# Moving seven small load requests from ScalarE's queue to SP's in a decode kernel

## The chip, the cores and the metric

The kernel runs on one core of a Trainium2 chip. A core has a matrix engine (TensorE, PE), whose weight loads are listed separately (PEld), a vector engine (VectorE, DVE), an activation engine (ScalarE, ACT), GpSimd (POOL) and SyncE (SP). Transfers from the chip's main memory (HBM) into the core's memory are carried out by 16 DMA engines, and they are requested by instructions on SP or on ScalarE. The metric is the device time of one execution in microseconds (us); the median over several runs counts.

## The reference

One token of a decoder: attention over a long cache, a small token mixer, and a gate that blends the two.

```python
x = A_x                                              # [1, 1, 448]
g = sigmoid((x * gate_w).sum(-1, keepdims=True))     # one number

q = (x @ wq)                                         # wq [448, 4096]: 16 heads of 256
k, v = k_cache, v_cache                              # 8 heads, 65536 rows of 256 each; 2 query heads share one
p = softmax(q . k * 256 ** -0.5)
a = (p . v) @ wo                                     # wo [4096, 448]

h = layernorm(x)
u = gelu(h * w1 + b1)                                # w1, b1: 1792 numbers each; u is [448, 1792]
b = u @ w2 + b2                                      # w2: 1792 numbers, b2: one

out = g * a + (1 - g) * b
```

All inputs are bf16. The two caches are 268 MB each; everything else is small beside them.

## The kernel before

**Blocks.** Each of the 8 cache heads is cut into 4 blocks of 16384 rows, 8 MiB of keys and 8 MiB of values each: 32 blocks. For a block, VectorE transposes the keys (`transposes`, L410), TensorE forms the scores (`scores`, L418), a softmax step follows (`softmax`, from L475), and TensorE multiplies the probabilities with the values (`pv`, L438). A running maximum and a running denominator carry from block to block.

**The loop.** `For_i` at L605 runs 15 times over two blocks each. The last two blocks stand behind the loop, written out, with the last values loaded in seven pieces (`load_v_last`, L161). All engines meet at the loop's entry. In the loop SP requests the values of a block (`load_v`, L135) and then the keys of the next one (`load_k_whole`, L132); it waits for a place to come free ahead of each. The very first keys are requested ahead of the loop, the first values inside it.

**Places in memory.** The keys live in `k_all`, three half-block slots; block 0 takes the first two. The third slot is used before the loop as room for the mixer (`gel`, `xf`, `h_bc`, `zt`). The values live in `vt`. Before the first values come, `vt` holds `wq`: its first 384 rows (`wq_m`, 3 MiB) and the last 64 (`wq_t`, 512 KiB).

**Order.** Every instruction goes through `seq`, which ties it to the one before it on its engine, so that an engine's work runs in the order written. The start-up is written in this order:

- The loads. ScalarE requests x (`xr`, L166), three tables of 14 rows (`w1`, `b1` and `w2`, L176), the gate's weights in two halves (`gw`, L178) and b2 (`b2b`, L181). SP requests `wq_t` (L167), `wq_m` (L170) and the first keys (L132).
- Constants on GpSimd and VectorE (L185 to L226).
- x is brought into columns and spread over 128 rows by TensorE (L237 to L245), which needs `xr` and the constant `ones_b` (L212).
- One product turns the tables into columns (L263). VectorE copies the result out (L273, L274), directly after the first statistics of the layer norm, and then takes two Newton steps for the reciprocal root (L277 to L282) and forms `h_bc` (L283).
- ScalarE takes 14 Gelus from `h_bc` and the tables (L288).
- TensorE forms q from `wq` and x (L299, L306); it is spread into `qz` (L317 to L332).
- The gate's sum is taken (L346 to L348: it needs `gw`, and its Exp stands behind the Gelus on ScalarE), and TensorE sums the mixer (L352).
- `mixer_tail` (L357 to L368, which needs `b2b`) is written behind the loop, but in the trace it runs on VectorE before the loop is entered.

**Semaphores of the loads.** The ten loads ahead of the loop share eight semaphores in turn. A load that takes over the semaphore of an earlier one waits until that one has landed: the ninth for the first, the tenth for the second. The order of taking them follows the order of the loads: x, `wq_t`, the rest, with b2 as the ninth and the first keys as the tenth.

Of the kernel before, what the change touches and what calls it, by code (L numbers as in the profile page):

```python
# [33 lines left out]
def kernel(  # L34
# [15 lines left out]
    nc = tc.nc  # L50
# [5 lines left out]
    NF = F // 128  # L56
# [6 lines left out]
    def seq(ins):  # L63
        e = ins.ins.engine
        if e in last:
            tc.add_manual_dep(
                ins.ins,
                last[e],
                mybir.DependencyInfo(
                    mybir.DependencyClass.NoSync, mybir.DependencyReason.DATA  # L70
                ),
                reason="program order",
            )
        last[e] = ins.ins.name
        return ins
# [29 lines left out]
    xr = const.tile([1, D], BF16)  # L105
    gw = const.tile([1, D], BF16)
    tables = const.tile([3 * NF, 128], BF16)
    w2b = const.tile([128, NF], BF16)
    b2b = const.tile([1, 1], BF16)
# [21 lines left out]
    def load_k_whole(n, slot):  # L131
        seq(nc.sync.dma_start(out=k_all[:, slot * KP:(slot + 2) * KP, :], in_=rows("k", n)))  # L132
# [26 lines left out]
    def load_v_last(n):  # L159
# [3 lines left out]
                in_=rows("v", n)[:, j0:j1, :],  # L163
            ))

    seq(nc.scalar.dma_start(out=xr[:], in_=A_x[0, 0].rearrange("(o n) -> o n", o=1)))  # L166
    seq(nc.sync.dma_start(  # L167
        out=wq_t[:, :], in_=A_wq[DM:D, :].rearrange("r (h n) -> (r h) n", h=2)
    ))
    seq(nc.sync.dma_start(out=wq_m, in_=A_wq[0:DM, :].rearrange("(p k) n -> p k n", k=3)))  # L170
    for k, table in enumerate((
        B_w1[0].rearrange("(b p) -> b p", p=128),
        B_b1.rearrange("(b p) -> b p", p=128),
        B_w2.rearrange("(b p) o -> b (p o)", p=128),
    )):
        seq(nc.scalar.dma_start(out=tables[k * NF:(k + 1) * NF, :], in_=table))  # L176
    for n0, n1 in ((0, D // 2), (D // 2, D)):
        seq(nc.scalar.dma_start(  # L178
            out=gw[:, n0:n1], in_=gate_w.rearrange("(o n) -> o n", o=1)[:, n0:n1]
        ))  # L180
    seq(nc.scalar.dma_start(out=b2b[:], in_=B_b2.rearrange("(o n) -> o n", o=1)))  # L181
    load_k_whole(0, 0)


# [9 lines left out]
        out=val[:], in_=rowsel[:, :, :, 0:NI], op=ALU.add, axis=AXIS.XY  # L194
    ))
    fst = const.tile([128, 2, REP], FP32)
    for e in range(2):
        seq(nc.vector.tensor_reduce(
            out=fst[:, e, :], in_=rowsel[:, :, :, e:e + 1], op=ALU.add, axis=AXIS.XY
# [3 lines left out]
        out=par[:], in_=ident_f[:].rearrange("p (a r) -> p r a", r=REP), op=ALU.add, axis=AXIS.X  # L203
# [3 lines left out]
        out=nval[:], in0=val[:], scalar1=-scale, scalar2=None, op0=ALU.mult  # L207
# [7 lines left out]
        out=same[:], in_=val[:].unsqueeze(1).to_broadcast([128, 64, REP])  # L215
# [8 lines left out]
        out=sel[:],  # L224
        in_=ident.rearrange("p (w k) -> p w k", w=NW).unsqueeze(2).to_broadcast([128, NW, NQ, 32]),
# [7 lines left out]
        out=xrr[:], in_=xr[:, DM:D].unsqueeze(2).to_broadcast([1, D - DM, 2])  # L233
    ))
    x_col = hd_ps[:, 40:44]
    for k in range(3):
# [13 lines left out]
        out=xtm[:], in0=par[:], scalar1=x_col[:, 3:4], scalar2=None, op0=ALU.mult  # L250
# [19 lines left out]
        out=veps[:], in0=mv[:, 1:2], scalar1=1e-5, scalar2=None, op0=ALU.add  # L270
# [5 lines left out]
    for _ in range(2):  # L276
# [3 lines left out]
            out=ntmp[:], in0=ntmp[:], scalar1=-0.5, scalar2=1.5, op0=ALU.mult, op1=ALU.add  # L280
# [3 lines left out]
        out=h_bc, in0=xf, scalar1=mv[:, 0:1], scalar2=rstd[:, 0:1],  # L284
        op0=ALU.subtract, op1=ALU.mult,
    ))
    for b in range(NF):
        seq(nc.scalar.activation(  # L288
            out=gel[b], in_=h_bc, func=ACT.Gelu_apprx_tanh,
# [33 lines left out]
    for k in range(2):  # L323
        seq(nc.vector.tensor_copy(
            out=qq[:, :, :, k, :], in_=qq_ps.rearrange("p (w g r) -> p w g r", g=HKV, r=REP)
# [314 lines left out]
    for n in (L - 1, L):  # L640
# [14 lines left out]
        else:  # L655
            def rest_base():
# [9 lines left out]
                out=lsv[:], in0=val[:], scalar1=lsum[:, 0:1], scalar2=None, op0=ALU.mult  # L666
# [8 lines left out]
                out=rdv[:], in0=rdv[:], scalar1=gcol[:, 0:1], scalar2=None, op0=ALU.mult  # L675
# [6 lines left out]
    for c in range(2):  # L682
# [9 lines left out]
        out=oT[:], in0=o_last, in1=rdv[:].unsqueeze(1).to_broadcast([128, 2, REP]), op=ALU.mult  # L692
# [43 lines left out]
```

## Time and profile before

| | us |
|---|---|
| median of 3 runs | 1264.22 |
| lowest and highest | 1263.58, 1266.26 |
| span of the profiled execution | 1261.8 |
| TensorE busy | 824.5 |
| VectorE busy | 711.8 |
| ScalarE busy | 75.7 |

The profiled execution is given by its span, from its first instruction to its last, 1261.8 us; the runs' times, taken without the profiler, have a median 2.4 us above it. Of the bytes, 544.22 MB are read from HBM, a mean of 431 GB/s over the span.

How to read the lines: the page of a profile cuts the span into 40 equal slices and gives for each the busy share in tenths or the GB/s moved. A timeline row has the start and the length in us, the engine (with a q where it is the engine's sequencer, as in a request), the line of the kernel, the operation, what it writes and reads, and in brackets how long the engine had been idle before it and what ended that. A row of issues ends with the us from the request to the landing. A row of packets counts the pieces in which the DMA engines move data, each at its start; a transfer ends on every engine that takes part in it with a packet of 4 bytes.

### The profile page before, as it was taken

How to read it: one execution, taken by the hardware profiler on the slowest of the kernel's cores; microseconds unless marked ns; L12 is line 12 of the kernel's file. 1: busy time of each engine (PE TensorE's matmuls, PEld its weight loads, DVE VectorE, ACT ScalarE, POOL GpSimd, SP SyncE). 2: the span in 40 equal slices, each digit the busy share in tenths (PEclk: the TensorE clock that was granted, in tenths of full speed). 3: DMA queues.
4: the chain of work that ended last, by engine and by line, in shares of the span. 5: the costliest groups of instructions: out<-in, count | busy, mean ns of one | idle time of the engine just before them, and what ended most of it. 6: DMA issues, size and time to landing. Idle time of an engine off the chain costs nothing.

```text
span 1261.8 us, 12358 instructions
## 1 busy us (share of the span) xinstructions
PE 824.5 (65%) x4818; PEld 331.2 (26%) x4818; DVE 711.8 (56%) x755; ACT 75.7 (6%) x163; POOL 4.8 (0%) x9
## 2 busy tenths in 40 slices
PE   4757467575666756577566766658656576665668
PEld 2222122222222312223222322223222232222224
DVE  5665456654556644566544665445655456654575
ACT  4000000000000000000000000000000000000000
POOL 1000000000000000000000000000000000000000
PEclk8887788877787877978778887788877797877878
DMA  9999999999999999999999999999999999999998
GB/s 415 435 435 432 439 432 432 437 434 437 432 434 435 434 425 440 416 441 443 423 434 437 432 432 439 432 439 432 432 439 432 439 432 432 439 432 435 421 435 355
DMA packets 11624, 544.36 MB, mean 431 GB/s; under 512 B 1532, under 2 KB 1918, under 8 KB 2782
## 3 DMA queue, kind: packets, MB, share of 16 engines
q1 hardware_dynamic: 11522, 544.22, 99.6%
q8 instruction: 6, 0.10, 0.0%
q14 instruction: 4, 0.03, 0.0%
q10 hardware_dynamic: 92, 0.01, 0.0%
HBM read 544.22 MB, written 0.00 MB: 431 GB/s over the span
## 4 chain that ended last, share of the span: by engine, by line
DMA 67%; PE 14%; DVE 13%; issue 4%; ACT 0%; SPq 0%; DVEq 0%; ACTq 0%
DMA k_all<-in_A_k_cache_dram 67%; PE sc L418 13%; DVE kT L410 13%; PE hd_ps L463 0%; PE pv_last L438 0%; PE pv_last L563 0%; PE f L563 0%; DVE rmax L475 0%; PE hd_ps L684 0%; ACT p_sb L506 0%; PE hd_ps L554 0%; PE pv_ps L438 0%; PE f L697 0%; PE sm_ps L493 0%; DVE pT L513 0%
## 5 line engine op out<-in xcount | busy, mean ns | idle before, releaser
L418 PE MATMUL sc<-kT,qz 128*128 128x512 bf16 x2048 | 550.4, 419 | 315.0 <-DVE kT L410 314.8
L410 DVE STREAM_TRANSPOSE kT<-k_all 128x2048 f32<-128x2048 f32 x256 | 571.3, 2283 | 207.6 <-DMA k_all<-in_A_k_cache_dram 154.7
L418 PEld LDWEIGHTS <-qz 128*128 128x128 bf16 x2048 | 212.5, 104 | 651.3 <-issue 474.8
L438 PE MATMUL pv_ps<-vt,pT 128*4 128x512 bf16 x1968 | 172.0, 525 | 27.3 <-DVE pT L513 27.3
L519 DVE SCALAR_TENSOR_TENSOR acc<-acc,al,pv_ps 128x512 f32<-128x512 f32 x31 | 23.2, 747 | 160.4 <-PE pv_ps L438 160.4
L438 PEld LDWEIGHTS <-pT 128*4 128x4 bf16 x2000 | 56.5, 108 | 130.1 <-issue 83.9
L506 ACT ACTIVATE p_sb<-sc,nb 128x512 bf16<-128x512 f32 x32 | 22.0, 687 | 1020.0 <-DVE nb L502 1020.0
L475 DVE TENSOR_REDUCE rmax<-sc 128x1 f32<-128x512 f32 x32 | 22.1, 692 | 63.7 <-PE sc L418 63.7
L513 DVE STREAM_TRANSPOSE pT<-p_sb 128x512 bf16<-128x512 bf16 x32 | 22.8, 712 | 27.1 <-ACT p_sb L506 27.1
L525 PE MATMUL hd_ps<-lsum,same 128*128 128x1 f32 x30 | 8.2, 342 | 28.8 <-DVE lsum L514 28.8
L493 PE MATMUL sm_ps<-mrun,ones_f 1*128 1x2 f32 x64 | 12.1, 256 | 21.2 <-DVE mrun L492 13.0
L479 PE MATMUL sm_ps<-ident_f,rmax 128*1 128x128 f32 x32 | 8.6, 270 | 24.5 <-DVE rmax L475 24.5
L563 PE MATMUL pv_last<-wo_in,steps 128*128 128x448 bf16 x64 | 15.6, 368 | 5.5 <-PEq L605 5.5
L563 PEld LDWEIGHTS <-steps 128*128 128x128 bf16 x128 | 11.6, 101 | 22.6 <-issue 14.4
L493 PEld LDWEIGHTS sm_ps<-mrun,ones_f 1*128 1x128 f32 x64 | 9.4, 182 | 27.4 <-DVE mrun L492 16.3
L567 ACT CAST wo_sb<-pv_last 128x448 bf16<-128x448 f32 x16 | 8.5, 532 | 126.3 <-PE pv_last L563 126.3
L558 DVE TENSOR_TENSOR a_acc<-a_acc,hd_ps 1x448 f32<-1x448 f32 x15 | 9.1, 608 | 12.3 <-PE hd_ps L554 12.3
L554 PE MATMUL hd_ps<-wo_sb,oT 128*1 128x448 bf16 x60 | 15.8, 351 | 0.0
L563 PE MATMUL f<-wo_in,steps 128*128 128x448 bf16 x64 | 15.5, 367 | 0.0
L570 ACT COPY wo_sb<-wo_sb 128x896 bf16<-128x896 bf16 x15 | 14.1, 937 | 14.5 <-PE hd_ps L554 14.5
L525 PEld LDWEIGHTS hd_ps<-lsum,same 128*128 128x128 f32 x30 | 6.9, 285 | 30.1 <-DVE lsum L514 30.1
L550 DVE CAST oT<-hd_ps 128x2 bf16<-128x2 f32 x15 | 2.4, 160 | 20.8 <-PE hd_ps L540 20.8
(124 smaller groups left out, 194.6 us busy)
## 6 DMA issues: line engine op xcount, KB each, us to landing
k_all<-in_A_k_cache_dram SPq DMA_DIRECT2D x2, 4096.0 KB, 15.2
vt<-in_A_v_cache_dram SPq DMA_DIRECT2D x1, 5120.0 KB
k_all<-in_A_v_cache_dram SPq DMA_DIRECT2D x1, 4096.0 KB
wo_in<-in_A_wo_dram SPq DMA_DIRECT2D x15, 224.0 KB, 27.8
vt<-in_A_wq_dram SPq DMA_DIRECT2D x1, 3072.0 KB, 10.4
vt<-in_A_v_cache_dram SPq DMA_DIRECT2D x1, 3072.0 KB
k_all<-in_A_v_cache_dram SPq DMA_DIRECT2D x1, 2048.0 KB
k_all<-in_A_v_cache_dram SPq DMA_DIRECT2D x1, 1024.0 KB, 21.7
```

What stands on the lines that cost most here:

```text
L410: seq(nc.vector.transpose(out=kT_tiles[i % 2][:].rearrange("p j w k c -> p (j w k c)").bitcast(FP32), in_=slots[pair[i // 4]][:, i % 4 * N ...
L418: seq(nc.tensor.matmul(sc_tiles[e][:, :], lhsT=qz[:, 2 * w + c, 2 * (NI - i):2 * (NI - i) + 128], rhs=kT_tiles[i % 2][:, :, w, :, c], star ...
L438: seq(nc.tensor.matmul(dst[32 * grp:32 * grp + 2 * REP, :, :], lhsT=pT[:, 32 * jj + 2 * REP * ip:32 * jj + 2 * REP * (ip + 1)], rhs=pairs( ...
L475: seq(nc.vector.tensor_reduce(out=rmax[:], in_=sc_ps[:, :], op=ALU.max, axis=AXIS.X))
L493: seq(nc.tensor.matmul(sm_ps[:, 128:128 + REP], lhsT=ones_f[0:1, :], rhs=mrun[0:1, :], start=True, stop=True))
L506: seq(nc.scalar.activation(out=p_sb[:, :], in_=sc_ps[:, :], func=ACT.Exp, scale=scale, bias=nb[:, 0:1], accum_out=den[:, 0:1],))
L513: seq(nc.vector.transpose(out=pT[:, :], in_=p_sb[:, :]))
L519: seq(nc.vector.scalar_tensor_tensor(out=acc[:], in0=acc[:], scalar=al_tiles[e][:, 0:1], in1=src[:, :, :], op0=ALU.mult, op1=ALU.add,))
L525: seq(nc.tensor.matmul(hd_ps[:, 460:461], lhsT=same[:].rearrange("p a r -> p (a r)"), rhs=lsum[:, 0:1], start=True, stop=True,))
L554: seq(nc.tensor.matmul(a_ps, lhsT=oT[:, c, r:r + 1], rhs=wo_sb[:, r, c, :], start=(r == 0 and c == 0), stop=(r == REP - 1 and c == 1),))
L563: seq(nc.tensor.matmul(wo_ps[c], lhsT=steps[:, WS - u:WS - u + 128], rhs=wo_in[:, 2 * u + c, :], start=(u == 0), stop=(u == WS - 1),))
L570: seq(nc.scalar.copy(out=wo_sb[:, 0], in_=wo_sb[:, 1]))
```

## The change

All seven requests of ScalarE are made by SP. x moves from ahead of both parts of `wq` to between them; the tables, the gate's weights and b2 stand, in their old order, behind the large part of `wq` and ahead of the first keys. ScalarE requests nothing any more.

```diff
-    seq(nc.scalar.dma_start(out=xr[:], in_=A_x[0, 0].rearrange("(o n) -> o n", o=1)))
     seq(nc.sync.dma_start(
         out=wq_t[:, :], in_=A_wq[DM:D, :].rearrange("r (h n) -> (r h) n", h=2)
     ))
+    seq(nc.sync.dma_start(out=xr[:], in_=A_x[0, 0].rearrange("(o n) -> o n", o=1)))
     seq(nc.sync.dma_start(out=wq_m, in_=A_wq[0:DM, :].rearrange("(p k) n -> p k n", k=3)))
     for k, table in enumerate((
         B_w1[0].rearrange("(b p) -> b p", p=128),
         B_b1.rearrange("(b p) -> b p", p=128),
         B_w2.rearrange("(b p) o -> b (p o)", p=128),
     )):
-        seq(nc.scalar.dma_start(out=tables[k * NF:(k + 1) * NF, :], in_=table))
+        seq(nc.sync.dma_start(out=tables[k * NF:(k + 1) * NF, :], in_=table))
     for n0, n1 in ((0, D // 2), (D // 2, D)):
-        seq(nc.scalar.dma_start(
+        seq(nc.sync.dma_start(
             out=gw[:, n0:n1], in_=gate_w.rearrange("(o n) -> o n", o=1)[:, n0:n1]
         ))
-    seq(nc.scalar.dma_start(out=b2b[:], in_=B_b2.rearrange("(o n) -> o n", o=1)))
+    seq(nc.sync.dma_start(out=b2b[:], in_=B_b2.rearrange("(o n) -> o n", o=1)))
     load_k_whole(0, 0)
```

## The prediction

> **What bounds the kernel now.** I read the page first: span, engine shares, the slices, the rows by queue. Then the issues with their landing times, and last the requests and the order of work of the first 30 us, the only place the diff touches.
>
> The page: span, slices, rows by queue.
>
> ```profile
> span 1261.8 us, 12358 instructions
> DMA  9999999999999999999999999999999999999998
> GB/s 415 435 435 432 439 432 432 437 434 437 432 434 435 434 425 440 416 441 443 423 434 437 432 432 439 432 439 432 432 439 432 439 432 432 439 432 435 421 435 355
> q1 hardware_dynamic: 11522, 544.22, 99.6%
> q10 hardware_dynamic: 92, 0.01, 0.0%
> ```
>
> Two queues carry data: q1 (11522 packets, 544.22 MB) and q10 (92 packets, 0.01 MB). SP's requests are the megabytes, so q1 is SP's and q10 ScalarE's. q1's packets take 99.6% of the 16 engines' span: the transfers bound the kernel, and other work counts only where it lets the stream run dry or makes it start late.
>
> The issues of the first 40 us; the last number is us from request to landing.
>
> ```profile
> vt<-in_A_wq_dram SPq DMA_DIRECT2D x1, 3072.0 KB, 10.4
> vt<-in_A_wq_dram SPq DMA_DIRECT2D x1, 512.0 KB, 3.2
> k_all<-in_A_k_cache_dram SPq DMA_DIRECT2D x1, 28.1
> vt<-in_A_v_cache_dram SPq DMA_DIRECT2D x1, 24.3
> ```
>
> The requests in the timeline: start, length.
>
> ```profile
> 0.74 0.42 SPq L167 DMA_DIRECT2D vt<-in_A_wq_dram  x1
> 1.22 0.41 SPq L170 DMA_DIRECT2D vt<-in_A_wq_dram  x1
> 3.98 0.33 SPq L132 DMA_DIRECT2D k_all<-in_A_k_cache_dram  x1
> 27.07 0.35 SPq L135 DMA_DIRECT2D vt<-in_A_v_cache_dram  x1
> 0.74 0.53 ACTq L166 DMA_DIRECT2D xr<-in_A_x_dram  x1
> 1.30 0.34 ACTq L176 DMA_DIRECT2D tables<-in_B_w_dram  x1
> 3.45 0.26 ACTq L181 DMA_DIRECT2D b2b<-in_B_b_dram  x1
> ```
>
> Landings: small part of wq 0.74 + 3.2 = 3.9; large part 1.22 + 10.4 = 11.6; first K block 3.98 + 28.1 = 32.1; first V block 27.07 + 24.3 = 51.4. V lands 19.3 us after K: the stream's pace for 8 MiB. From here the order on q1 is fixed, so whatever moves K's landing by d moves the end by d, if V is requested in time.
>
> **The change part by part.** Seven requests leave ScalarE for SP. The bytes stay the same.
>
> *SP's time.* A request costs SP 0.48 us (1.22 - 0.74). x goes between the two parts of wq, so the large part is requested at about 1.70 instead of 1.22. Then six small ones: K would be requested at 1.70 + 7 x 0.43 (ScalarE's own spacing, (3.45 - 1.30) / 5 = 0.43), about 4.7. Before, SP sat still ahead of K:
>
> ```profile
> SPq L132 <- DMA vt<-in_A_wq_dram: 2.3, 1, 2.3
> SPq L605 <- PEq L605: 21.5, 1, 21.5
> ```
>
> 2.3 us were a wait for the small part of wq: the tenth request takes over the second one's semaphore. With the new order the ninth (b2) waits for wq's small part, landed at 3.9 and so over when SP gets there at 4.3, and the tenth (K) for x, requested at 1.22 behind 512 KB. No new waiting. K's request 0.7 us later is hidden: the wq data ahead of it run until 11.6.
>
> *The large part of wq, 0.48 later.* This one may not be hidden. The window of the first 3.3 us (its 40 slices and its packets, each counted where it starts), and the packets from 3.3 to 3.7:
>
> ```profile
> GB/s 0 0 0 0 0 0 0 0 0 0 0 0 0 0 0 0 0 0 0 0 11 99 348 199 298 149 298 298 397 546 298 447 447 348 496 348 447 298 149 199
> DMA packets 133, 0.50 MB, mean 153 GB/s; under 512 B 9, under 2 KB 10, under 8 KB 133
> DMA packets 29, 0.41 MB, mean 1034 GB/s; under 512 B 8, under 2 KB 8, under 8 KB 13
> ```
>
> The small part's data start in the 22nd slice, at 21 x 0.0825 = 1.7 to 1.8, 1.0 us after their request (the slice before holds x). Before 3.3 all 133 packets are under 8 KB: nothing of the large part. Afterwards 16 of 29 are larger: the large part begins on all 16 engines between 3.3 and 3.7, at the earliest 2.1 us after its request. By 3.3 nine packets under 512 B had started: x's closing one and eight of the small part's sixteen, one for each engine that is through with it. So half the engines were waiting for the large part. If 2.1 us from request to first packet holds, it begins at 3.8: 0.1 to 0.5 later than now, engine by engine. Bounds: 0 (the 2.1 us was only the queue ahead of it) and 1.0 (x holds the generation of transfers a further 0.5 us, one whole request, besides the 0.48). I take 0.3, the middle of what the engines' own starts give, and this goes to the end.
>
> *x.* Requested at 1.22 and landing behind wq's small part, about 4. Its covers:
>
> ```profile
> 2.03 0.10 PEld L237 LDWEIGHTS <-xr 1*128 1x128 bf16 x1 [2.03 <-DMA xr<-in_A_x_dram]
> 6.38 0.22 PE L237 MATMUL hd_ps<-ones_b,xr 1*128 1x1 bf16 x3 [6.38 <-DVE ones_b L212]
> 7.66 0.20 DVE L232 COPY xrr<-xr 1x128 bf16<-1x128 bf16 x1
> ```
>
> The weights load at 2.03, but the product waits for ones_b until 6.38. So 2.4 us of cover; cost 0. Gone, each us past 6.38 would be one us on VectorE's chain below.
>
> *The tables.* Now they stand behind 3 MB instead of in a queue of their own. Work that needs them, in order:
>
> ```profile
> 10.03 0.19 PE L263 MATMUL hd_ps<-steps,tables 42*128 42x42 bf16 x1 [1.54 <-DVE mv L268]
> 10.26 0.19 DVE L273 COPY wb<-hd_ps 128x28 f32<-128x28 f32 x1
> 11.69 0.24 PE L299 MATMUL hd_ps<-xm,vt 128*128 128x1 bf16 x3 [1.47 <-DMA vt<-in_A_wq_dram]
> 12.24 0.51 DVE L283 TENSOR_SCALAR k_all<-k_all,mv,rstd 128x448 f32<-128x448 f32 x1
> 12.79 9.23 ACT L288 ACTIVATE k_all<-k_all,wb 128x448 bf16<-128x448 f32 x14 [1.02 <-DVE k_all L283]
> 23.33 0.20 ACT L348 ACTIVATE ez<-z 1x1 f32<-1x1 f32 x1
> 25.30 0.61 DVE L368 TENSOR_TENSOR rest<-y_sb,rest 1x448 f32<-1x448 f32 x1
> 27.18 1.67 PE L563 MATMUL pv_last<-wo_in,steps 128*128 128x448 bf16 x4 [4.70 <-PEq L605]
> ```
>
> Tables land just after wq, 11.6 + 0.3 + 0.1 = 12.0, and L263 runs at 12.1 instead of 10.03: 2.1 us later. L273 stands behind it on VectorE and the Newton steps, L283, the 14 Gelus, the Exp and the gate's tail follow without slack to 25.91 (L368's end). On TensorE the q products (L299) now queue behind L263: from 11.69 to 12.3, 0.6 us, hidden, since they end 3.4 us later and the Gelus end at 24.1. So the loop's entry, at which SP waited 21.5 us for the others, is 2.1 us later, and V is requested at 27.07 + 2.1 = 29.2.
>
> Cover for that: V must be there when an engine has finished K. Large packets that start about there, in the window 29.9 to 30.8:
>
> ```profile
> DMA packets 31, 0.99 MB, mean 1101 GB/s; under 512 B 15, under 2 KB 15, under 8 KB 15
> ```
>
> 15 closing packets: 15 of the 16 engines finish K between 29.9 and 30.8 now, the last by its landing at 32.1. With wq 0.3 later: 30.2 to 31.1. V's first packet comes 1.0 to 2.1 us after its request (the two parts of wq), so at 30.2 to 31.3. Engines that finish first may stand dry, by 0 to 1.1 us; the slowest does not. Only the slowest sets K's and V's landing, but engines delayed here have less in hand later. I take 0.2 for it, of 0 to 0.7.
>
> *Gate weights and b2.* They land right behind the tables, before K. L346 needs gw at 19.12, L361 b2 at 23.82: cost 0, over 6 us of cover.
>
> *ScalarE.* It gets its first table load 3 us earlier; Sqrt waits for VectorE until 10.26. Gain 0. q10's 92 packets no longer cut in between q1's: 92 short packets over 16 engines, nothing measurable.
>
> *Later.* The next K is requested when block 0's transposes free its place; they start 2.1 us later, and V then has five more us to run. In the loop the requests have this room:
>
> ```profile
> DMA to landing us min/median/max: 24.3/26.8/29.7
> ```
>
> V's 32 requests land 26.8 us after they are made, against 19.3 us of transfer: 7.5 us in hand, and the minimum, 24.3, is the first one, with 5.0. One late start is absorbed there.
>
> Sum: +0.3 (wq) + 0.2 (V) = +0.5 us: span 1261.8 to 1262.3. The execution's span is 2.4 us under the median of the runs, 1264.22; nothing of the change lies there. Predicted 1264.7.
>
> A rule against this sum: by the Trainium skill (DMA: Bandwidth & Descriptors, Queues, rings and completion order) an engine takes turns between the queues it has work for and keeps the ring's order inside one queue. The trace agrees as far as it goes: the tables were used at 10.03, before the large part landed at 11.6, though requested after it. By the rule the tables come behind wq, which is the 2.1 us above; without it they would still be used at 10.03 and the sum would be +0.3.
>
> **The rivals.**
>
> *The small transfers hold the queue one by one (slower).* If each of six small ones on q1 has to be finished before the next begins, each costs what x took from request to use, 2.03 - 0.74 = 1.3 us, and the stream stands for 6 x 1.3 = 7.8 us ahead of K: 1264.2 + 7.8 = 1272. It decides from 2 such waits on. Against it: short packets follow each other on q1 without a gap in the last stage, window 1250 to 1256:
>
> ```profile
> DMA packets 577, 2.42 MB, mean 403 GB/s; under 512 B 67, under 2 KB 203, under 8 KB 417
> ```
>
> 577 packets, 203 of them under 2 KB, still 403 GB/s. By the same page of the Trainium skill (Anatomy of one DMA) a transfer has a fixed part of some 2 us on the GpSimd path, most of it the receipt of the last write; an estimate by that figure is 12 us if nothing of it overlapped. The row above agrees that packets behind do not wait for it.
>
> *V comes too late (slower).* If the tables are usable three landings later than I say, each x's 1.3 us, V is asked for 3.9 us later, at 33.1, and its first packet comes at 34.1 to 35.2. The slowest engine is done with K at 32.4, so all stand for 1.7 to 2.8 us: 1264.2 + 0.3 + 2.3 = 1266.8. It decides once V is asked for after about 31. For it: the first V has the least room of all 32. Against: as above.
>
> *The engines come out more even (faster).* K took 32.1 - 11.6 = 20.5 us after wq where V takes 19.3. One engine fetched instructions in between:
>
> ```profile
> q8 instruction: 1, 0.02, 5.5%
> ```
>
> That is 5.5% of 16 us in the 1 us from 17.5 on, 0.9 us on one engine. Should such fetches fall on engines that are ahead, the end is up to 1.2 us earlier: 1263.0. Nothing in the change aims at it.
>
> *Nothing at all.* wq's delay and V's both hidden: 1264.2.
>
> **How the numbers follow.** Chances: forecast (with "nothing at all" as its lower edge) 0.73, more even 0.13, V late 0.08, queue held 0.06. The forecast's own range is 1263.4 to 1265.9 (+1.0 and +0.7 at most). The runs before spread from 1263.58 to 1266.26, 0.2%, which is about what a measurement of this kernel can tell from no change: 2.5 us. The range reaches down to 1262.6 and up to 1267.2, into the late V, and leaves the held queue out. Within 0.2% (1261.7 to 1266.7): 0.84. Slower: held queue, half of the late V, and 0.03 of spread, 0.13. Faster: 0.03, since the even engines alone do not reach it.
>
> **What would show it.** L263 at 12.0 to 12.3 right ahead of L299, L288 from about 14.9, V's request at about 29.2, K requested at 4.7 and landing at 32.2 to 32.6, V 19.3 to 19.8 us later, later V requests unchanged against their landings. q10 gone. It is wrong if K lands after 34 (a held queue), if V lands more than 20.5 us after K (dry), or if the loop's pace of 38.6 us for a K and a V differs.

## The result and the profile after

The changed kernel takes 1265.80 us (median of 21 runs, 1264.53 to 1267.75) against 1263.91 us for the kernel before on the same chip (21 runs). The ratio is 1.0017, 95% interval 1.001 to 1.0023: slower by about 1.9 us. The ratio here and below is taken over all the runs, so it need not equal the quotient of the two medians. The forecast was +0.5 us.

The page of the kernel after: span, slices, queue.

```profile
span 1263.9 us, 12359 instructions
DMA  9999999999999999999999999999999999999998
GB/s 406 409 439 431 439 431 431 439 431 437 433 431 439 431 437 433 431 437 433 437 433 436 432 433 437 431 439 431 433 437 431 439 431 431 439 431 439 412 434 360
q1 hardware_dynamic: 11614, 544.23, 99.6%
```

q10 is gone; its 92 packets are now part of q1's 11614. The span is 2.1 us longer (1261.8 before). The first two slices, 31.6 us each, moved 406 and 409 GB/s where they had moved 415 and 435. So the time went at the beginning, and the rest of the stream runs as before.

The requests on SP in the first 50 us, from the timeline:

```profile
0.73 0.42 SPq L166 DMA_DIRECT2D vt<-in_A_wq_dram  x1
1.21 0.31 SPq L169 DMA_DIRECT2D xr<-in_A_x_dram  x1
1.57 0.34 SPq L170 DMA_DIRECT2D vt<-in_A_wq_dram  x1
5.01 0.35 SPq L132 DMA_DIRECT2D k_all<-in_A_k_cache_dram  x1
30.28 0.37 SPq L135 DMA_DIRECT2D vt<-in_A_v_cache_dram  x1
47.48 0.34 SPq L132 DMA_DIRECT2D k_all<-in_A_k_cache_dram  x1
```

And the work that leads to V's request:

```profile
13.32 0.19 PE L263 MATMUL hd_ps<-steps,tables 42*128 42x42 bf16 x1 [4.83 <-DMA tables<-in_B_w_dram]
16.00 9.22 ACT L288 ACTIVATE k_all<-k_all,wb 128x448 bf16<-128x448 f32 x14 [4.24 <-DVE k_all L283]
26.54 0.20 ACT L348 ACTIVATE ez<-z 1x1 f32<-1x1 f32 x1
28.51 0.61 DVE L368 TENSOR_TENSOR rest<-y_sb,rest 1x448 f32<-1x448 f32 x1
30.29 1.67 PE L563 MATMUL pv_last<-wo_in,steps 128*128 128x448 bf16 x4 [4.42 <-PEq L605]
```

Each stands 3.1 to 3.3 us later than before: L263 13.32 for 10.03, the Gelus 16.00 for 12.79, the gate's last step 28.51 for 25.30, V's request 30.28 for 27.07. L263 now waits for the tables themselves, for 4.83 us.

What that did to the DMA engines: packets that start in two windows around the change from the first K block to the first V block, with the share of 16 engines that they take.

```profile
DMA packets 13, 0.01 MB, mean 11 GB/s; under 512 B 12, under 2 KB 12, under 8 KB 12
DMA packets 16, 0.92 MB, mean 1668 GB/s; under 512 B 2, under 2 KB 2, under 8 KB 2
q1 hardware_dynamic: 16, 0.92, 498.2%
```

The first row is 30.5 to 31.25: 12 engines close K with their short packet, and no packet of V starts anywhere. They stand dry. In the second, 31.25 to 31.8, 14 of V's large packets start, the first of them 1.0 us after the request. They also take longer: 498.2% of 16 x 0.55 us is 43.8 us, 3.1 us each. The same count for the kernel before, later in its first V block, 32.4 to 33.1:

```profile
DMA packets 14, 0.92 MB, mean 1311 GB/s; under 512 B 0, under 2 KB 0, under 8 KB 0
q1 hardware_dynamic: 14, 0.92, 302.6%
```

302.6% of 16 x 0.7 us over 14 packets is 2.4 us each. V's own first packets in the kernel before, which follow K without a gap (30.0 to 30.7), are not slow either:

```profile
q1 hardware_dynamic: 30, 0.98, 332.7%
```

Of these 30 packets 15 are short ones that close K; 332.7% of 16 x 0.7 us over the other 15 is 2.5 us each. So most engines lost some tenths of a us standing, in the mean about 0.7 (an estimate from windows of 0.1 us), and then 0.6 us in a slow first packet.

The second K block shows the sum. Request and landing time, before and after:

```profile
k_all<-in_A_k_cache_dram SPq DMA_DIRECT2D x1, 26.7
```

```profile
k_all<-in_A_k_cache_dram SPq DMA_DIRECT2D x1, 25.0
```

Before it lands at 43.98 + 26.7 = 70.7, after at 47.48 + 25.0 = 72.5: 1.8 us late, almost the whole 1.9 us of the result. I use this landing below as the mark of what the beginning cost. It is not the whole of it: 0.3 us more is added in the next 80 us (the fourth K lands at 148.39 before and 150.54 after). Then nothing is, as two later K blocks in the chain that ended last show (start and length), before and after:

```profile
198.28 27.92 DMA k_all<-in_A_k_cache_dram
...
1132.73 27.27 DMA k_all<-in_A_k_cache_dram
```

```profile
200.44 27.93 DMA k_all<-in_A_k_cache_dram
...
1134.70 27.48 DMA k_all<-in_A_k_cache_dram
```

They land at 226.20 and 1160.00 before, at 228.37 and 1162.18 after: 2.2 us late in both. In between, over 930 us, the stream neither wins nor loses in these two executions.

### The profile page after: what moved, and what is told of

The parts are those of the page before. It is cut to its first block, busy times and chain, and to the rows that moved or that the text cites. A ratio compares the mean times of both kernels' runs of the same rounds, so it can differ in the third digit from the quotient of the medians.

```text
span 1263.9 us, 12359 instructions
## 1 busy us (share of the span) xinstructions
PE 821.9 (65%) x4818; PEld 330.5 (26%) x4818; DVE 711.4 (56%) x755; ACT 75.6 (6%) x163; POOL 4.8 (0%) x9
## 4 chain that ended last, share of the span: by engine, by line
DMA 68%; PE 13%; DVE 12%; issue 4%; SPq 0%; ACT 0%; DVEq 0%
DMA k_all<-in_A_k_cache_dram 67%; DVE kT L410 12%; PE sc L418 12%; DMA k_all<-in_A_v_cache_dram 2%; PE pv_last L563 0%; PE hd_ps L554 0%; PE f L563 0%; SPq L161 0%; PE sm_ps L540 0%; ACT p_sb L506 0%; PE f L697 0%; DVE rmax L475 0%; SPq L132 0%; PE hd_ps L540 0%; PE sm_ps L493 0%
## 5 line engine op out<-in xcount | busy, mean ns | idle before, releaser
L513 DVE STREAM_TRANSPOSE pT<-p_sb 128x512 bf16<-128x512 bf16 x32 | 22.8, 712 | 27.1 <-ACT p_sb L506 27.1
L493 PE MATMUL sm_ps<-mrun,ones_f 1*128 1x2 f32 x64 | 12.1, 256 | 21.2 <-DVE mrun L492 13.0
L563 PEld LDWEIGHTS <-steps 128*128 128x128 bf16 x128 | 11.6, 101 | 22.5 <-issue 14.3
L525 PEld LDWEIGHTS hd_ps<-lsum,same 128*128 128x128 f32 x30 | 6.3, 262 | 30.1 <-DVE lsum L514 30.1
## 6 DMA issues: line engine op xcount, KB each, us to landing
vt<-in_A_wq_dram SPq DMA_DIRECT2D x1, 3072.0 KB, 10.9
```

The source lines that it names most:

```text
L493: seq(nc.tensor.matmul(sm_ps[:, 128:128 + REP], lhsT=ones_f[0:1, :], rhs=mrun[0:1, :], start=True, stop=True))
L513: seq(nc.vector.transpose(out=pT[:, :], in_=p_sb[:, :]))
L525: seq(nc.tensor.matmul(hd_ps[:, 460:461], lhsT=same[:].rearrange("p a r -> p (a r)"), rhs=lsum[:, 0:1], start=True, stop=True,))
L563: seq(nc.tensor.matmul(wo_ps[c], lhsT=steps[:, WS - u:WS - u + 128], rhs=wo_in[:, 2 * u + c, :], start=(u == 0), stop=(u == WS - 1),))
```

## The experiments

Theory A: the tables come late, so V is asked for too late, and the engines run dry ahead of it. Theory B: the large part of wq begins late, because it is requested later. Later two more: C, a short transfer between the two parts of wq is what costs; D, x on SP's queue costs wherever it stands. Medians are compared with runs of the kernel before on the same chip.

**Only x moves.**

```diff
-    seq(nc.scalar.dma_start(out=xr[:], ...))
     seq(nc.sync.dma_start(out=wq_t[:, :], ...))
+    seq(nc.sync.dma_start(out=xr[:], ...))
     seq(nc.sync.dma_start(out=wq_m, ...))
```

> Only x moves: SP requests it between the two parts of wq; the tables, the gate's weights and b2 stay with ScalarE. Theory A (the first V block is requested too late, because the tables come late, and the DMA engines run dry ahead of it): the tables arrive by about 10, L263 near 10 to 10.5, V requested at 27 to 27.6, no dry stretch; time within 0.5 us of the kernel before, ratio 1.000 to 1.0004. Theory B (the loss is the late start of wq's large part): wq lands about 0.9 us later, 12.5 instead of 11.6, and nearly the whole loss is here, +1.5 to +2 us, ratio 1.0012 to 1.0017.

1264.95 us against 1263.96: ratio 1.0008, interval 0.9999 to 1.0017. V was requested at 27.05, and the second K landed at 70.7 as before. So in the profiled execution nothing was lost up to there: B's late wq is not what costs the changed kernel its 1.8 us by the second K. But the runs spread from 1263.65 to 1266.34, where those of the kernel before lie between 1263.63 and 1264.45. The interval does not settle whether the median rose.

**Only the six small ones move.**

```diff
-        seq(nc.scalar.dma_start(out=tables[...], in_=table))
+        seq(nc.sync.dma_start(out=tables[...], in_=table))
 (and the same for gw and b2b; x stays with ScalarE)
```

> Only the six small requests move to SP, behind wq's large part; x stays with ScalarE, so that part is requested at 1.22 as before. Theory A: L263 at 12 to 13.3, V requested at 29 to 30.3, 10 or more engines dry ahead of V; +0.8 to +2 us, ratio 1.0006 to 1.0016. Theory B: wq lands at 11.6 as before; 0 to +0.3 us, ratio 1.000 to 1.0003.

1265.66 us against 1263.96: ratio 1.0013, interval 1.0004 to 1.0022, and the runs lie within 1.0 us. As A expects. The rows of its profile:

```profile
12.22 0.19 PE L263 MATMUL hd_ps<-steps,tables 42*128 42x42 bf16 x1 [3.74 <-DMA tables<-in_B_w_dram]
29.20 0.37 SPq L135 DMA_DIRECT2D vt<-in_A_v_cache_dram  x1
k_all<-in_A_k_cache_dram SPq DMA_DIRECT2D x1, 25.5
```

V is requested 2.1 us late, the lateness of my forecast (L263 at 12.1, V at 29.2), and it costs 1.7 us, not 0.2. The window 30 to 33, in which each of the 16 engines closes K and starts one packet of V:

```profile
DMA packets 33, 1.06 MB, mean 352 GB/s; under 512 B 16, under 2 KB 16, under 8 KB 16
q1 hardware_dynamic: 32, 1.05, 97.0%
```

97.0% of 16 x 3 us over 16 large packets is 2.9 us each, 0.4 above the 2.5 of the kernel before. In windows of 0.1 us, 15 engines close K between 30.1 and 30.7, but eight of them begin V only between 30.7 and 31.8, up to 2.5 us after the request. From these windows I estimate that an engine stood for 0.6 us in the mean. Together that is 1.0 us per engine. The second K, requested at 46.35, lands at 71.8, 1.2 us late; the K that lands at 1160.00 before lands at 1161.77 here, 1.8 us late. So the loss goes on growing after 72 us, until 189, and for that part no cause is shown.

**The changed kernel with a shorter chain to the loop.**

```diff
-    for b in range(NF):
+    for b in range(NF - 5):
         seq(nc.scalar.activation(out=gel[b], in_=h_bc, ...))
 (and 9 instead of 14 products in mixer_sum)
```

> The changed kernel with 9 of the 14 Gelus and 9 of the 14 products that sum them (the mixer's sum is left incomplete): 5 x 0.66 = 3.3 us less on the chain to the loop's entry; all requests as in the changed kernel. Theory A: V requested at about 27.0 again, no dry stretch, V lands 19.3 us behind K; the loss falls to what wq's start costs, 0 to +0.8 us, ratio 1.000 to 1.0006. Theory B: the loss stays, ratio 1.0014 to 1.0018.

V was requested at 27.05 again and the second K landed at 70.8; the profiled span is 1262.4. There A holds. The runs do not follow: 1265.51 us against 1263.96, ratio 1.0014, interval 1.0005 to 1.0023, spread from 1264.19 to 1267.08. With x between the two parts and V in time, something else cost 1.5 us in the median, and more than 1 us in eight of the eleven runs.

**The kernel before with a longer chain.**

```diff
-    for b in range(NF):
+    for b in [NF - 1] * 5 + list(range(NF)):
         seq(nc.scalar.activation(out=gel[b], in_=h_bc, ...))
```

> The kernel before with five Gelus repeated (19 instead of 14, the extra ones into the last tile ahead of the real ones): 3.3 us more on the chain to the loop's entry, all requests as before. Theory A: V requested at 30.3 to 30.4 as in the changed kernel, the engines dry for up to 1.3 us ahead of V, and +1 to +2 us, ratio 1.0008 to 1.0016. Theory B: nothing, ratio 1.000 to 1.0003.

1266.34 us against 1263.96: ratio 1.0023, interval 1.0014 to 1.0032, a little above what A said. No request ahead of the loop was touched. V is asked for at 30.88. In its window 30.2 to 31.8 all but one of the engines close K and none begins V:

```profile
DMA packets 16, 0.01 MB, mean 5 GB/s; under 512 B 15, under 2 KB 15, under 8 KB 15
q14 instruction: 1, 0.01, 1.2%
```

So lateness of V alone, with ScalarE still requesting everything it used to, makes a loss of the size of the changed kernel's. B is not needed for it.

**Two bytes between the parts of wq.**

```diff
     seq(nc.sync.dma_start(out=wq_t[:, :], ...))
+    seq(nc.sync.dma_start(out=b2b[:], ...))
     seq(nc.sync.dma_start(out=wq_m, ...))
 (b2b no longer requested by ScalarE)
```

> The kernel before with the two bytes of b2 requested by SP between the two parts of wq; x, the tables and the gate's weights stay with ScalarE. The large part is requested at about 1.55 instead of 1.22, and V at 27.0. Theory C (a short transfer on one engine between the two parts is what costs, whatever it carries): as with x there, a median 0.5 to 1.5 us above the kernel before, ratio 1.0004 to 1.0012, and runs that spread over more than 2 us. Theory D (it was x itself, by what waits for it): ratio 0.9998 to 1.0003, runs within 1 us.

1264.17 us against 1263.90: ratio 1.0003, interval 0.9994 to 1.0012; runs from 1263.56 to 1265.77, ten of the eleven within 1.2 us. Below C's median, with one run as far out as C says. Undecided between C and D.

**x on SP, but first.**

```diff
-    seq(nc.scalar.dma_start(out=xr[:], ...))
+    seq(nc.sync.dma_start(out=xr[:], ...))
     seq(nc.sync.dma_start(out=wq_t[:, :], ...))
```

> The kernel before with x requested by SP, but ahead of both parts of wq, which then follow each other directly; the rest stays with ScalarE. Both parts are requested 0.4 to 0.5 us later. Theory C (a transfer between the two parts costs): runs within 1 us of each other and +0.3 to +0.6 us for the later start, ratio 1.0002 to 1.0005. Theory D (x on SP's queue costs, wherever): the spread of over 2 us and +1 us or more, ratio 1.0008 to 1.0014.

1264.20 us against 1263.90: ratio 1.0002, interval 0.9993 to 1.0011, runs from 1263.80 to 1264.85. D is not borne out: x on SP's queue does not spread the runs when it does not stand between the two parts, though the interval still reaches 1.0011. The +0.3 us is what C allowed for the later start, but by the interval it is not told from zero. In the profile both parts of wq are requested 0.3 to 0.4 us later than before, and the stream is late by 0.46 us at the second K (71.12 for 70.66) and at 1160 (1160.46 for 1160.00). By this run that is what the later request costs by itself, a quarter of the changed kernel's loss.

**The six small ones on SP, with a shorter chain.** The edits of the second and third experiments together.

> The six small requests on SP behind wq and x on ScalarE, with 9 of the 14 Gelus and of the products that sum them (the mixer's sum is left incomplete): the chain to the loop's entry is 3.3 us shorter, the requests ahead of it are the same. Theory A (V is asked for too late and the engines run dry): V requested at about 26, no dry stretch, K and V land as in the kernel before; ratio 0.9997 to 1.0003. If the small transfers on SP's queue cost by themselves: ratio 1.0008 to 1.0015 stays.

1263.93 us against 1263.90: ratio 1.0000, interval 0.9991 to 1.0009. The tables are as late as in the second experiment, but V is asked for at 26.58:

```profile
12.26 0.19 PE L263 MATMUL hd_ps<-steps,tables 42*128 42x42 bf16 x1 [3.77 <-DMA tables<-in_B_w_dram]
26.58 0.37 SPq L135 DMA_DIRECT2D vt<-in_A_v_cache_dram  x1
DMA packets 31, 0.99 MB, mean 1239 GB/s; under 512 B 15, under 2 KB 15, under 8 KB 15
```

The last row is 30.0 to 30.8: 15 closing packets and 15 of V's large ones, each engine going straight on. So the six requests cost nothing measurable by themselves, neither on SP's time nor in the queue. Their price is V's request.

**The kernel before with V about as late as the six small ones make it.** Three repeated Gelus instead of five.

> The kernel before with three Gelus repeated: 2.0 us more on the chain to the loop's entry, all requests ahead of it as before. V requested at 29.0 to 29.3, as with the six small requests on SP (29.2). Theory A: the same loss as there, +1.2 to +1.8 us, ratio 1.0009 to 1.0014. Theory B or small transfers that cost by themselves: 0 to +0.3 us.

1266.12 us against 1263.90: ratio 1.0015, interval 1.0006 to 1.0024. The median is 2.2 us up, a little more than A said. V at 29.41, second K requested at 46.89 and landed 25.0 later, at 71.9: within 0.1 us of the same place as with the six small requests on SP (71.8). The intervals of the two overlap almost wholly. Same cause, made in another way.

**The two parts of wq exchanged.** An attempt at a better version than both.

```diff
+    seq(nc.sync.dma_start(out=wq_m, ...))
     seq(nc.sync.dma_start(out=wq_t[:, :], ...))
-    seq(nc.sync.dma_start(out=wq_m, ...))
```

> The kernel before with SP's first two requests exchanged: the large part of wq at 0.74, the small one at 1.22; ScalarE's requests as before. In the kernel before half the engines stood still for 0.1 to 0.4 us at 3.2 to 3.6 because the large part was not ready; with it in front, 7 us of transfer cover the small part's request. A gain of 0 to 0.4 us, ratio 0.9997 to 1.0000, if all engines begin the large part together near 1.8; none, or a loss, if its beginning takes 2 us from the request in any place.

1265.92 us against 1264.07: ratio 1.0015, interval 1.0006 to 1.0024. Neither outcome I had listed came about; SP's own waits show why:

```profile
SPq L132 <- DMA vt<-in_A_wq_dram: 8.7, 1, 8.7
SPq L168 <- DMA xr<-in_A_x_dram: 0.8, 1, 0.8
```

K, the tenth load, takes over the semaphore of the second, which is now the large part. So K is requested only at 11.03, when the large part has landed. The packets of the small part get fewer from about 11.2 on, and K's first packets start at 12.0: the engines run dry. K lands at 33.9 instead of 32.1. These 1.8 us account for the loss of 1.85: another dry queue, passed on. The second row shows that the small part had to wait as well: requested at 2.02 and not at 1.22, once x had landed. A wait for the first load is what the ninth has, so it seems that the semaphores are not always taken in the order in which the loads are written.

**Two more executions.** The third and the first experiment's kernels again, unchanged, for a second profile of each.

> The changed kernel with nine Gelus once more, unchanged, for a profile of another execution: its runs went from 1264.2 to 1267.1 and the one profiled was of the fastest. Theory C (x between the two parts): a slower execution has engines that begin the large part late, at 4 us or after, so that wq's closing packets spread over 1.3 us or more instead of 0.6 to 0.9, and its K or V blocks land late from there on. Otherwise the start is like that of the fast one, and the time is lost after 80 us, in packets that take longer.

> The kernel before with x alone moved, once more, unchanged, for a profile of another execution (its runs went from 1263.7 to 1266.3). Same two possibilities as for the changed kernel with nine Gelus: late engines at wq's large part, or slower packets after 80 us.

They took 1263.63 and 1263.84 us, one run each, as fast as the kernel before, and their starts are clean: V requested at 26.58 and 27.05, second K landed at 70.9 in both. No execution of the slow sort was caught. The nearest is the first profile of the kernel with x alone moved, span 1262.7: its K blocks land 0.2 us late at 110 (109.97 for 109.78) and 0.55 late at 149 (148.94 for 148.39). The window 110 to 130 us of it, and of the kernel before:

```profile
DMA packets 144, 8.39 MB, mean 419 GB/s; under 512 B 16, under 2 KB 16, under 8 KB 16
```

```profile
DMA packets 150, 8.78 MB, mean 439 GB/s; under 512 B 16, under 2 KB 16, under 8 KB 16
```

Six large packets fewer in 20 us, though the ends of the window cut through blocks, so the landings are the better measure. Nor is this a mark of x's place: with the six small requests on SP and x on ScalarE the lateness grows in the same stretch from 1.2 to 1.5 us, and to 1.75 by 189. The page of the changed kernel has its dip in the second slice, but there the dry V is mixed in. Why a short transfer between the two parts should lead to this, and only in some executions, I have not settled.

**SP requests everything, x first.**

```diff
+    seq(nc.sync.dma_start(out=xr[:], ...))
     seq(nc.sync.dma_start(out=wq_t[:, :], ...))
-    seq(nc.sync.dma_start(out=xr[:], ...))
```

> The changed kernel with x ahead of both parts of wq: SP still requests everything, but no transfer stands between the two parts. Stream and tables 0.4 to 0.5 us later than with x on ScalarE, so L263 at 12.5 to 12.8, V requested at 29.4 to 29.8, K's blocks finished 0.4 us later too. Theory A alone (only V's late request costs, and x's place does not): a loss of 1.3 to 2.0 us, as with the six small requests on SP, ratio 1.0010 to 1.0016. Theory C (the transfer between the two parts adds the spread): runs within 1.2 us of each other instead of 3.2. If the runs still spread over 2.5 us or more, x's place is not where the changed kernel's spread comes from.

1265.92 us against 1264.00: ratio 1.0015, interval 1.0006 to 1.0024, the same as the changed kernel within the interval, and runs from 1265.22 to 1266.52, 1.3 us instead of 3.2. V's lateness (requested at 29.68, second K landed at 47.54 + 25.4 = 72.9) accounts for most of the median, as A says; by the profiles, the K near 1160 is 2.25 us late here, where the six small requests alone make 1.77 and x in front alone 0.46. The narrower spread is what C says. C is not shown by that: among the kernels with nothing between the two parts, the one with 19 Gelus spread over 2.6 us as well, three of its eleven runs 1.3 us or more above the other eight.

The next table puts the kernels together, in us. The first three columns of numbers come from one profiled execution each, the last from all runs. The third is the lateness of the K block that lands at 1160.00 in the kernel before.

| | V requested | second K landed | K near 1160 later by | median less that of before |
|---|---|---|---|---|
| before | 27.07 | 70.7 | 0 | 0 |
| six small on SP, 9 Gelus | 26.58 | 70.8 | 0.17 | 0.0 |
| x first on SP | 27.06 | 71.1 | 0.46 | +0.3 |
| b2 between the parts | 27.06 | 71.3 | 0.88 | +0.3 |
| x between the parts | 27.05 | 70.7 | 0.63 | +1.0 |
| changed kernel, 9 Gelus | 27.05 | 70.8 | 0.09 | +1.5 |
| parts exchanged (first K late) | 28.25 | 72.7 | 2.23 | +1.9 |
| six small on SP | 29.20 | 71.8 | 1.77 | +1.7 |
| before, 17 Gelus | 29.41 | 71.9 | 1.91 | +2.2 |
| all on SP, x first | 29.68 | 72.9 | 2.25 | +1.9 |
| changed kernel | 30.28 | 72.5 | 2.18 | +1.9 |
| before, 19 Gelus | 30.88 | 73.2 | 2.50 | +2.4 |

In the profiles the stream is 0.1 to 0.9 us late where V is requested by 27.1, and 1.8 to 2.5 where it is requested at 29.2 or later; the kernel with the parts exchanged, whose first K is late, stands apart. In the medians the two kernels with x between the parts and V in time do not fit: their profiled executions were faster than their median. The two losses do not add either. The six small requests alone make +1.7, x between the parts with V in time makes +1.0 and +1.5, and the changed kernel, which has both, +1.9. So V's late request is shown to be enough for the loss, and it is what the profiled execution of the changed kernel lost most of its time by. What x's place adds to it in the other runs is open.

No version beats the kernel before.

## Why the prediction was right or wrong

The sum had two terms, +0.3 for wq's start and +0.2 for V. The time lies in the range and within 0.2%, the sign is right, the size is a quarter of what was measured. That the time lies in the range owes something to its width: 1262.6 to 1267.2 was drawn for the spread of the runs and a late V as well. The term that was mis-sized is V's.

*SP's time.* Right. Small requests took 0.25 to 0.41 us each, except the two halves of the gate's weights (1.41 us together), K was requested at 5.01 instead of my 4.7, and no new semaphore wait appeared. K's later request was hidden.

*x.* Right that its landing is covered: the product at 6.38 did not move. I had not seen that its place between the two parts could spread the runs.

*The large part of wq.* I took +0.3, bounds 0 to 1.0. In the profile after it landed at 1.57 + 10.9 = 12.5, 0.9 late and near the upper bound (the row is 10.9 us for the 3072 KB); with x alone moved, the first K landed where it had before. With x ahead of both parts the delay stays, the stream is 0.46 us late to the end and the median is 0.3 up. The term's size was reasonable; its variation from run to run was not foreseen.

*The tables.* The mechanism was right, step by step: tables behind wq, L263, the Newton steps, the Gelus, the gate's tail, the loop's entry, V. The delay was 3.2 us rather than 2.1. 0.6 of the difference is wq's landing, later than I had it. The rest is that the tables were usable 0.8 us after wq had landed (12.5 to 13.3), where I had 0.1 to 0.2. With the six small requests alone, wq on time, the delay was the forecast 2.1; there is luck in that, since wq landed at 11.6, without the 0.3 that I had added, and the tables were usable 0.6 us later. The rule of the Trainium skill that a queue keeps its order on each engine (DMA: Bandwidth & Descriptors, Queues, rings and completion order) is borne out: the tables came right behind wq. They were used at 13.32, wq had landed at 12.5, and in a queue of their own they had been used at 10.03.

*V.* This is the step that failed. I worked out that V's first packet would come at 30.2 to 31.3 and the engines would finish K between 30.2 and 31.1. With the six small requests alone, where V is requested at the forecast 29.2, that is about what happened: 15 engines finish K at 30.1 to 30.7, and V's first packets start at 30.3 to 31.8. But I then let only the slowest engine count and took 0.2 of 0 to 0.7. The 5.0 us in hand that I read off the first V's landing are the slowest engine's, too: the first engine was through with K at 30.0, 3 us after V's request. The second and the seventh experiment measure the term by itself: 1.7 us with the forecast lateness of 2.1, nothing without it. Two things were missing. A first packet behind a dry stretch is slow: 3.1 us instead of 2.4 on 14 engines of the changed kernel, 2.9 in the mean with the six small requests. And an engine with time in hand at 31 us is not safe later. The engines lost 1.0 us in the mean at the start; the second K was 1.2 us late, and from 189 us on K was 1.75 late. How the lateness grows in between is not shown.

*The rivals.* "V comes too late" is what happened, but I gave it 0.08 and put its threshold at a request after 31. It costs 1.7 us at 29.2 already. "The small transfers hold the queue" is refuted by the ratio of 1.0000 with the six of them on SP and V in time. "More even" did not show. The reservation that engines delayed here have less in hand later was right, and I priced it too low.

## What to carry to other kernels

In a kernel that the transfers bound, look for the request with the least time in hand and follow every chain that leads to it: here three small tables, moved behind 3 MB, reached a request 17 us later through a matrix product, a few vector steps, 14 Gelus and a loop's entry. Price a queue that runs dry by what all its engines lose and not by the slowest alone, and at more than the gap: the first packets after it were slow too, and here 1.0 us lost per engine at the start went with a kernel that was 1.7 us longer. And when the order of loads is changed, see which semaphore each takes over: exchanging two of them made a third wait 8.7 us.

## What I had not expected of the hardware

Packets of 64 KiB that start after a dry stretch took about 3.1 us where the stream's take 2.4. With 19 Gelus, too, eleven of V's first packets take 3.2 us each (743.0% of 16 x 0.3 us, 31.8 to 32.1); those of the kernel before and of the six small requests with V in time, which follow K without a gap, take 2.5. Why the packets after a dry stretch are slow is not shown. Once the beginning is over, the stream keeps its pace to within 0.01 us over 930 us (2.17 and 2.18 us late), so that what is lost in the first 200 us is still lost at 1160.

The other surprise is open. With x between the two parts of wq, runs of the same program spread rather evenly over 2.7 us (x alone), 2.9 us (x, nine Gelus) and 3.2 us (the changed kernel). With b2 there they spread over 2.2 us, but ten of the eleven lie within 1.2. With none between, they lie within 0.7 to 1.5 us in six kernels tried (six small on SP with and without the shorter chain, x first on SP alone and with all the others, 17 Gelus, the parts exchanged), and in two more, the kernel before and the one with 19 Gelus, most do, with two of 21 and three of eleven runs apart from the rest. With x between and nine Gelus the interval (1.0005 to 1.0023) says that the runs are longer; with x alone, or b2, it does not. By which mechanism, no profile here shows.
